# Decode attention with a dense block on one core: value sums in pairs, short last chunks, column output, and VectorE's scores by tensor_tensor_reduce

## The chip, the cores and the metric

The kernel runs on one core of one Trainium2 chip. Times are device microseconds (us) of that core. The kernel before takes 2061.26 us (median of 2 runs, 2060.8 to 2061.72). A difference counts as "faster" or "slower" when it is over 2%.

In the profile, PE is TensorE, PEld its weight load, DVE is VectorE, ACT is ScalarE, POOL is GpSimd, and SP is SyncE, which issues the loads here. L225 means line 225 of that kernel's file. The core's loads are shared by 16 DMA engines: the trace of before holds 8,616 landing records for 540 loads and stores, about 16 for each. What is said below of fetches, packets and landings is read from the traces.

## The reference, cut to what matters

```python
D, H, Sk, Dh, Dff = 640, 32, 32768, 192, 1536          # one query row, bf16
q = layernorm(x) @ wq                                   # [H, Dh]
scores = einsum("hd,hkd->hk", q, k_cache) * Dh ** -0.5  # k_cache [H, Sk, Dh]
p = softmax(scores)
o = einsum("hk,hkd->hd", p, v_cache)
h = x + o.reshape(H * Dh) @ wo
out = h + relu(layernorm(h) @ w1) @ w2
```

One query meets 32 heads of 32,768 keys and values. K and V are 32 x 32768 x 192 x 2 bytes x 2 = 805 MB; each is read once. Everything else is small.

## The kernel before

A chunk is 4,096 keys of one head: 128 partitions of 32 consecutive rows of 192 elements. There are 8 chunks a head, 256 in all. A K or V load is one DMA of 128 rows of 12,288 bytes.

```python
J = 32; CH = P * J; NC = Sk // CH      # 32 rows a partition, 4096 keys a chunk, 8 chunks a head
JP = 10; JD = J - JP                   # 10 rows' scores by PE, 22 by VectorE
kpool = ... bufs=5                     # five K tiles and five V tiles
...
def load_kv(g):
    h, c = divmod(g, NC)
    kt = kpool.tile([P, J * Dh], bf16, name="kt")
    nc.sync.dma_start(out=kt[:], in_=k_hd[h, c * CH:(c + 1) * CH, :].rearrange("(p j) d -> p (j d)", p=P))
    ...                                # the same for V
def scores_dve(g, mid=None):           # VectorE: one row of every partition per instruction (L225)
    ...
    for j in range(JD):
        if j == 4 and mid is not None:
            mid()                      # denominator of the head before
        st = scp.tile([P, Dh], bf16, name="st")
        nc.vector.scalar_tensor_tensor(out=st[:], in0=kt[:, j * Dh:(j + 1) * Dh], scalar=1.0, in1=qb[:],
                                       op0=A.mult, op1=A.mult, accum_out=sc[:, j:j + 1])
    return sc
def pv(g):                             # PE: value sums, one row per matmul (L245)
    ...
    for jj in range(J):
        ...
        nc.tensor.matmul(o[:], lhsT=p, rhs=vt[:, j * Dh:(j + 1) * Dh], ...)
...
for g in range(G):
    ...
    if c == 0 and h == H // 2:
        nc.sync.dma_start(out=w1_sb[:], in_=B_w1.rearrange("(c p) n -> p c n", p=P))
    if c == 0 and h == H // 2 + 1:
        nc.sync.dma_start(out=w2_sb[:], in_=B_w2.rearrange("(c p) n -> p c n", p=P))
    transposes(g)                      # PE turns the 10 rows that it scores itself: 15 transposes
    pv(g - 1); scores_pe(g); sc = scores_dve(g, ...); ...; exp_dve(g, sc)
```

The instruction streams are fully unrolled. The instructions themselves have to be fetched (248 packets on the two instruction queues, below).

The softmax here doesn't subtract the row's maximum and nothing guards it: scores larger than these inputs give would overflow.

## Time and profile before

| | before |
|---|---|
| time, span of the profiled run | 2061.26 us, 2060.4 us |
| VectorE busy, PE busy, ScalarE busy | 78%, 68%, 32% |
| granted TensorE clock (mean) | 0.835 |
| instruction fetches: queue 8 (16,384 B each), queue 14 (8,192 B each) | 130, 118 |
| last K or V packet ends | 2038.5 us |

The first fence is the page of the kernel before: busy time by engine, DMA rate in 40 equal slices, the two queues that carry instructions (packets, MB, share of 16 engines' span), and the group of VectorE's score instructions (busy us, mean ns, idle time before them and what ended it).

```profile
PE 1405.5 (68%) x16643; PEld 1193.5 (58%) x16643; DVE 1603.1 (78%) x11352; ACT 651.6 (32%) x1719; POOL 0.7 (0%) x6
...
GB/s 395 423 421 420 423 421 423 407 422 420 423 422 357 423 418 423 416 346 425 382 420 344 418 423 421 423 423 393 425 421 422 414 350 423 420 423 417 397 412 77
...
q8 instruction: 130, 2.13, 0.4%
q14 instruction: 118, 0.97, 0.1%
...
L225 DVE SCALAR_TENSOR_TENSOR st<-kt,qb 128x192 bf16<-128x192 bf16 x5632 | 1589.7, 350 | 306.7 <-DMA kt<-in_A_k_cache_dram 294.7
```

No compute engine is full, and what VectorE's score instructions wait for is nearly always K (294.7 of 306.7 us), so the loads look like the limit. (VectorE is idle 457 us in all; 132.8 us of the rest is a wait for PE, shown below.) Yet they are not always at 423 GB/s: there are holes (357, 346, 344, 350). The table by stretches shows what a hole is; its columns are the stretch, its length, busy time and instruction count of PE, PEld, DVE, ACT and POOL, the granted clock, the DMA share and GB/s.

```profile
1040.00:1060.00 20.00, 14.24 (x175) 11.83 (x172) 14.91 (x106) 5.51 (x17) 0.00 (x0) 0.83 1.01 422
1080.00:1100.00 20.00, 12.32 (x160) 10.75 (x157) 14.49 (x103) 5.50 (x15) 0.00 (x0) 0.84 0.57 212
...
2020.00:2040.00 20.00, 14.73 (x165) 12.47 (x166) 17.06 (x121) 6.63 (x14) 0.00 (x0) 0.83 0.07 27
```

At 1080 us the rate halves, and from 2020 to 2040 us, with the last K and V still on their way, it is 27 GB/s: 423 / 16 = 26.4, the rate of one engine. Fifteen of the 16 DMA engines have finished their shares and one has not. The landing records of the last K load show the same: 15 of its 16 lie between 2013.34 and 2015.21 us, the last at 2035.28, and PE's work on it starts at 2035.33. So it is the last share that lets the compute engines start. With five tiles of each kind, the 15 others run ahead until no tile is free, and then stand idle: SyncE's queue waits 247.2 us for VectorE's scores before K loads and 208.4 us for PE's value sums before V loads. The single packets in the trace confirm this: over the whole kernel, 36.3 us pass before the last K or V packet in which at most one of the 16 engines moves data.

The chain of waits that ended last shows the tail (start, duration, what):

```profile
2005.22 30.06 DMA kt<-in_A_k_cache_dram
2035.28 0.05 issue
2035.33 1.01 PE tp L195 x15
2036.34 4.34 PE o_ps L245 x32
...
2041.56 2.80 PE o_ps L245 x32
...
2047.57 1.79 PE y_a L336 x8
...
2057.30 0.23 PE y_a L346
```

The last K lands at 2035.28 us and 25.1 us of dependent work follow. The waits of VectorE (us in total, times, longest) and a piece of its timeline (start, duration) complete the picture:

```profile
DVE st L225 <- DMA kt<-in_A_k_cache_dram: 294.7, 181, 5.7
DVE rec L258 <- PE den L252: 132.8, 32, 5.9
```

```profile
1000.16 0.35 DVE L225 SCALAR_TENSOR_TENSOR st<-kt,qb 128x192 bf16<-128x192 bf16 x1
1000.44 0.08 DVE L225 DVE_READ_ACCUMULATOR st<-kt,qb 128x1 f32 x1
1000.44 0.35 DVE L225 SCALAR_TENSOR_TENSOR st<-kt,qb 128x192 bf16<-128x192 bf16 x1
```

One score instruction of the program appears as two, the operation and a read of the accumulator, and one score starts 279 ns after the other (its pitch, the median over the trace). So 22 rows take 6.1 us of a chunk.

### The profile page before, as it was taken

How to read it: one execution, taken by the hardware profiler on the slowest of the kernel's cores; microseconds unless marked ns; L12 is line 12 of the kernel's file. 1: busy time of each engine (PE TensorE's matmuls, PEld its weight loads, DVE VectorE, ACT ScalarE, POOL GpSimd, SP SyncE). 2: the span in 40 equal slices, each digit the busy share in tenths (PEclk: the TensorE clock that was granted, in tenths of full speed). 3: DMA queues.
4: the chain of work that ended last, by engine and by line, in shares of the span. 5: the costliest groups of instructions: out<-in, count | busy, mean ns of one | idle time of the engine just before them, and what ended most of it. 6: DMA issues, size and time to landing. Idle time of an engine off the chain costs nothing. (4 is left out here: it accounts for less than half of the span.)

```text
span 2060.4 us, 48468 instructions
## 1 busy us (share of the span) xinstructions
PE 1405.5 (68%) x16643; PEld 1193.5 (58%) x16643; DVE 1603.1 (78%) x11352; ACT 651.6 (32%) x1719; POOL 0.7 (0%) x6
## 2 busy tenths in 40 slices
PE   5766666766667666666665666766677667677767
PEld 4555555655555555555555555555566556566555
DVE  6877887778787788777777778887778877788775
ACT  3333333333333233322322333332333323333332
POOL 0000000000000000000000000000000000000000
PEclk9888887788898788888888888898788987878787
DMA  9999999999999999989998999999999989999991
GB/s 395 423 421 420 423 421 423 407 422 420 423 422 357 423 418 423 416 346 425 382 420 344 418 423 421 423 423 393 425 421 422 414 350 423 420 423 417 397 412 77
DMA packets 87844, 828.10 MB, mean 402 GB/s; under 512 B 8619, under 2 KB 21420, under 8 KB 22060
## 3 DMA queue, kind: packets, MB, share of 16 engines
q1 hardware_dynamic: 87596, 825.00, 96.5%
q8 instruction: 130, 2.13, 0.4%
q14 instruction: 118, 0.97, 0.1%
HBM read 824.97 MB, written 0.00 MB: 400 GB/s over the span
## 5 line engine op out<-in xcount | busy, mean ns | idle before, releaser
L225 DVE SCALAR_TENSOR_TENSOR st<-kt,qb 128x192 bf16<-128x192 bf16 x5632 | 1589.7, 350 | 306.7 <-DMA kt<-in_A_k_cache_dram 294.7
L195 PE MATMUL tp<-ident_b,kt 128*128 128x128 bf16 x3840 | 335.3, 255 | 596.6 <-DMA kt<-in_A_k_cache_dram 596.6
L195 PEld LDWEIGHTS <-kt 128*128 128x128 bf16 x3840 | 280.5, 116 | 623.8 <-DMA kt<-in_A_k_cache_dram 623.8
L245 PE MATMUL o_ps<-vt,pA 128*1 128x192 bf16 x5632 | 606.0, 272 | 45.8 <-ACT pA L232 45.6
L245 PEld LDWEIGHTS <-pA 128*1 128x1 bf16 x5632 | 524.9, 95 | 106.4 <-ACT pA L232 55.9
L196 ACT COPY kT<-tp 128x1024 bf16<-128x1024 bf16 (+1 forms) x512 | 465.1, 960 | 347.6 <-PE tp L195 347.3
L225 DVE DVE_READ_ACCUMULATOR st<-kt,qb 128x1 f32 x5632 | 442.4, 79 | 0.1
L245 PE MATMUL o_ps<-vt,pB 128*1 128x192 bf16 x2560 | 354.6, 305 | 0.4 <-ACT pB L212 0.4
L245 PEld LDWEIGHTS <-pB 128*1 128x1 bf16 x2560 | 237.2, 101 | 73.2 <-issue 22.8
L212 ACT ACTIVATE pB<-sp 128x10 bf16<-128x10 f32 x256 | 46.3, 181 | 630.9 <-PE sp L209 627.3
L232 ACT ACTIVATE pA<-sc 128x22 bf16<-128x22 f32 x256 | 56.6, 221 | 397.0 <-DVE st L225 396.8
L205 PEld LDWEIGHTS <-kT 128*128 128x128 bf16 x1280 | 100.0, 96 | 44.2 <-issue 43.3
L205 PE MATMUL sp<-qm,kT 128*128 128x2 bf16 x1280 | 122.3, 166 | 0.4 <-ACT kT L196 0.4
L209 PE MATMUL sp<-qm,kT 128*128 128x1 bf16 x1280 | 118.8, 163 | 0.4 <-ACT kT L196 0.4
L207 PE MATMUL sp<-qm,kT 128*128 128x1 bf16 x1280 | 118.7, 163 | 0.0
L258 DVE TENSOR_REDUCE rec<-den 1x1 f32<-1x16 f32 x32 | 5.2, 162 | 132.8 <-PE den L252 132.8
L207 PEld LDWEIGHTS <-kT 128*128 128x128 bf16 x1280 | 102.6, 96 | 0.0
L209 PEld LDWEIGHTS <-kT 128*128 128x128 bf16 x1280 | 101.4, 95 | 0.5 <-ACT kT L196 0.5
L212 ACT ACTIVATION_READ_ACCUMULATOR pB<-sp 128x1 f32 x256 | 49.9, 195 | 0.1
L232 ACT ACTIVATION_READ_ACCUMULATOR pA<-sc 128x1 f32 x256 | 48.1, 188 | 0.1
L163 PE MATMUL qps<-wq,xn_ln 128*1 128x192 bf16 x160 | 18.7, 248 | 3.3 <-DMA wq<-in_A_wq_dram 3.3
L265 ACT ACTIVATE o_pair<-o_ps,rec 1x192 f32<-1x192 f32 x32 | 13.2, 413 | 8.3 <-DVE rec L259 8.3
(62 smaller groups left out, 145.8 us busy)
## 6 DMA issues: line engine op xcount, KB each, us to landing
kt<-in_A_k_cache_dram SPq DMA_DIRECT2D x256, 1536.0 KB, 30.5
vt<-in_A_v_cache_dram SPq DMA_DIRECT2D x256, 1536.0 KB, 29.0
wq<-in_A_wq_dram SPq DMA_DIRECT2D x8, 960.0 KB, 27.1
wo<-in_A_wo_dram SPq DMA_DIRECT2D x16, 480.0 KB, 28.2
w_sb<-in_B_w_dram SPq DMA_DIRECT2D x2, 1920.0 KB, 32.2
x_row<-in_A_x_dram SPq DMA_DIRECT2D x1, 1.2 KB
out_dram<-y_row SPq DMA_DIRECT2D x1, 1.2 KB
```

The lines of the kernel that those rows point to most:

```text
L163: nc.tensor.matmul(qps[:], lhsT=xnT[:, c:c + 1], rhs=wq[:, c, hh * Dh:(hh + 1) * Dh], start=(c == 0), stop=(c == DT - 1))
L195: nc.tensor.transpose(out=tp[:, b, :], in_=kt[:, off:off + P], identity=ident_b[:])
L196: nc.scalar.copy(out=kT[:, b0:b0 + nb, :], in_=tp[:, 0:nb, :])
L205: nc.tensor.matmul(sp[:, 2 * i:2 * i + 2], lhsT=kT[:, 3 * i + 1, :], rhs=qm[:, 1:3], start=True, stop=False, skip_group_check=True)
L207: nc.tensor.matmul(sp[:, 2 * i:2 * i + 1], lhsT=kT[:, 3 * i, :], rhs=qm[:, 0:1], start=False, stop=False, skip_group_check=True)
L209: nc.tensor.matmul(sp[:, 2 * i + 1:2 * i + 2], lhsT=kT[:, 3 * i + 2, :], rhs=qm[:, 3:4], start=False, stop=True, skip_group_check=True)
L212: nc.scalar.activation(out=pB[:], in_=sp[:], func=F.Exp, scale=SCALE, accum_out=dsums[:, h, 2 * c + 1:2 * c + 2])
L225: nc.vector.scalar_tensor_tensor(out=st[:], in0=kt[:, j * Dh:(j + 1) * Dh], scalar=1.0, in1=qb[:], op0=A.mult, op1=A.mult, accum_out=sc[:, ...
L232: nc.scalar.activation(out=pA[:], in_=sc[:], func=F.Exp, scale=SCALE, accum_out=dsums[:, h, 2 * c:2 * c + 1])
L245: nc.tensor.matmul(o[:], lhsT=p, rhs=vt[:, j * Dh:(j + 1) * Dh], start=(c == 0 and jj == 0), stop=(c == NC - 1 and jj == J - 1))
L258: nc.vector.reduce_sum(out=s[:, 0:1], in_=d[:], axis=mybir.AxisListType.X)
L265: nc.scalar.activation(out=o_pair[(h // 2) % 2][0:1, (h % 2) * Dh:(h % 2 + 1) * Dh], in_=o[:], func=F.Copy, scale=s[0:1, 1:2])
```

## The change

The intent is to halve PE's value matmuls (two rows to a matmul, 384 columns wide, of which the matching halves are used), to hand VectorE four more rows a chunk by `tensor_tensor_reduce` (26 instead of 22, so PE transposes 6 rows instead of 10), to shorten the tail by splitting the last K and V rows into smaller chunks and producing the output as a column, and to take w1 in quarters of 120 + 8 partitions. The last point presumably aims at the lagging DMA engine.

```diff
-    JP = 10
-    JD = J - JP
+        parts = [(J, 6)] * NC                       # (rows a partition, rows scored by PE)
+        if h == H - 1:
+            parts = [(J, 6)] * (NC - 2) + [(J, 10), (16, 6), (8, 4), (8, 4)]
...
-                if j == 4 and mid is not None:
+                if j == 2 and mid is not None:
...
-                nc.vector.scalar_tensor_tensor(out=st[:], in0=kt[:, j * Dh:(j + 1) * Dh], scalar=1.0, in1=qb[:],
-                                               op0=A.mult, op1=A.mult, accum_out=sc[:, j:j + 1])
+                nc.vector.tensor_tensor_reduce(out=st[:], in0=kt[:, j * Dh:(j + 1) * Dh], in1=qb[:], scale=1.0,
+                                               scalar=0.0, op0=A.mult, op1=A.add, accum_out=sc[:, j:j + 1])
...
-            for jj in range(J):
...
-                nc.tensor.matmul(o[:], lhsT=p, rhs=vt[:, j * Dh:(j + 1) * Dh],
+            order = list(range(JD, jc, 2)) + list(range(0, JD, 2))
+            for i, j in enumerate(order):
+                p = pA[:, j:j + 2] if j < JD else pB[:, j - JD:j - JD + 2]
+                nc.tensor.matmul(o[:], lhsT=p, rhs=vt[:, j * Dh:(j + 2) * Dh],
...
-            if c == 0 and h == H // 2:
-                nc.sync.dma_start(out=w1_sb[:], in_=B_w1.rearrange("(c p) n -> p c n", p=P))
-            if c == 0 and h == H // 2 + 1:
+            if c == 2 and h >= H // 2 and h < H // 2 + 4:
+                i = h - H // 2
+                n1 = Dff // 4
+                w1_view = B_w1.rearrange("(c p) n -> p c n", p=P)
+                nc.sync.dma_start(out=w1_sb[0:120, :, i * n1:(i + 1) * n1], in_=w1_view[0:120, :, i * n1:(i + 1) * n1])
+                nc.sync.dma_start(out=w1_sb[120:P, :, i * n1:(i + 1) * n1], in_=w1_view[120:P, :, i * n1:(i + 1) * n1])
+            if c == 2 and h == H // 2 + 4:
                 nc.sync.dma_start(out=w2_sb[:], in_=B_w2.rearrange("(c p) n -> p c n", p=P))
...
-        for f in range(FT):                          # second dense matmul, a row of 640: 24 wide matmuls
-            nc.tensor.matmul(y_a[:], lhsT=h1T[:, f:f + 1], rhs=w2_sb[:, f, 0:512], ...
+        for n in range(DT):                          # the same as a column: 60 one-column matmuls
+            for f in range(FT):
+                nc.tensor.matmul(yps[:, n:n + 1], lhsT=w2_sb[:, f, n * P:(n + 1) * P], rhs=h1T[:, f:f + 1], ...
```

More of the change, by code (lines that the diff above doesn't have):

```diff
@@ L41 @@
     J = 32
-    CH = P * J
-    NC = Sk // CH
-    G = H * NC
-    JP = 10
-    JD = J - JP
-    NB = JP * Dh // P
-    QG = 4
-    assert Sk % CH == 0 and 2 * Dh == 3 * P and JP % 2 == 0 and H % QG == 0 and H % 2 == 0
+    QG = 4
+    assert Sk % (P * J) == 0 and 2 * Dh == 3 * P and H % QG == 0 and H % 2 == 0
+    NC = Sk // (P * J)
+    chunks = []
+    for h in range(H):
+        parts = [(J, 6)] * NC
+        if h == H - 1:
+            parts = [(J, 6)] * (NC - 2) + [(J, 10), (16, 6), (8, 4), (8, 4)]
+        k0 = 0
+        for c, (jc, jp) in enumerate(parts):
+            chunks.append((h, c, k0, jc, jp))
+            k0 += P * jc
+        assert k0 == Sk
+    G = len(chunks)
+    NCH = [sum(1 for q in chunks if q[0] == h) for h in range(H)]
+    NCM = max(NCH)
+    NBM = max(q[4] for q in chunks) * Dh // P
     const = ctx.enter_context(tc.tile_pool(name="const", bufs=1))
@@ L94, in load_kv @@
     def load_kv(g):
-        h, c = divmod(g, NC)
+        h, c, k0, jc, jp = chunks[g]
         kt = kpool.tile([P, J * Dh], bf16, name="kt")
-        nc.sync.dma_start(out=kt[:], in_=k_hd[h, c * CH:(c + 1) * CH, :].rearrange("(p j) d -> p (j d)", p=P))
+        nc.sync.dma_start(out=kt[:, 0:jc * Dh],
+                          in_=k_hd[h, k0:k0 + P * jc, :].rearrange("(p j) d -> p (j d)", p=P))
         vt = vpool.tile([P, J * Dh], bf16, name="vt")
-        nc.sync.dma_start(out=vt[:], in_=v_hd[h, c * CH:(c + 1) * CH, :].rearrange("(p j) d -> p (j d)", p=P))
+        nc.sync.dma_start(out=vt[:, 0:jc * Dh],
+                          in_=v_hd[h, k0:k0 + P * jc, :].rearrange("(p j) d -> p (j d)", p=P))
         kt_t[g], vt_t[g] = kt, vt
@@ L110 @@
     nc.vector.memset(ones_row[:], 1.0)
-    ones_col = const.tile([P, 1], f32)
+    ones_col = const.tile([P, 2], f32)
     nc.vector.memset(ones_col[:], 1.0)
@@ L119 @@
         nc.vector.memset(r[:], 0.0)
-    dsums = const.tile([P, H, 2 * NC], f32)
+    dsums = const.tile([P, H, 2 * NCM], f32)
+    nc.vector.memset(dsums[:], 0.0)
     w1_sb = const.tile([P, DT, Dff], bf16)
     w2_sb = const.tile([P, FT, D], bf16)
-    o_pair = [const.tile([1, 2 * Dh], f32, name=f"o_pair{i}") for i in range(2)]
+    o_pair = [const.tile([2, 2, 2 * Dh], f32, name=f"o_pair{i}") for i in range(2)]
     attT = aps.tile([P, DT], f32, name="attT")
@@ L188, in transposes @@
             kt = kt_t[g]
-            kT = tsb.tile([P, NB, P], bf16, name="kT")
+            h, c, k0, jc, jp = chunks[g]
+            NB = jp * Dh // P
+            kT = tsb.tile([P, NBM, P], bf16, name="kT")
             for b0 in range(0, NB, 8):
@@ L193, in transposes @@
                 for b in range(nb):
-                    off = JD * Dh + (b0 + b) * P
+                    off = (jc - jp) * Dh + (b0 + b) * P
                     nc.tensor.transpose(out=tp[:, b, :], in_=kt[:, off:off + P], identity=ident_b[:])
@@ L200, in scores_pe @@
             kT = kT_t.pop(g)
-            h, c = divmod(g, NC)
+            h, c, k0, jc, JP = chunks[g]
             qm = qm_t[h]
-            sp = sps.tile([P, JP], f32, name="sp")
+            sp = sps.tile([P, J], f32, name="sp")
             for i in range(JP // 2):
@@ L210, in scores_pe @@
                                  start=False, stop=True, skip_group_check=True)
-            pB = pcp.tile([P, JP], bf16, name="pB")
-            nc.scalar.activation(out=pB[:], in_=sp[:], func=F.Exp, scale=SCALE,
+            pB = pcp.tile([P, J], bf16, name="pB")
+            nc.scalar.activation(out=pB[:, 0:JP], in_=sp[:, 0:JP], func=F.Exp, scale=SCALE,
                                  accum_out=dsums[:, h, 2 * c + 1:2 * c + 2])
@@ L217, in scores_dve @@
             kt = kt_t.pop(g)
-            h, c = divmod(g, NC)
+            h, c, k0, jc, jp = chunks[g]
+            JD = jc - jp
             qb = qb_t[h]
-            sc = scp.tile([P, JD], f32, name="sc")
+            sc = scp.tile([P, J], f32, name="sc")
             for j in range(JD):
-                if j == 4 and mid is not None:
+                if j == 2 and mid is not None:
                     mid()
                 st = scp.tile([P, Dh], bf16, name="st")
-                nc.vector.scalar_tensor_tensor(out=st[:], in0=kt[:, j * Dh:(j + 1) * Dh], scalar=1.0, in1=qb[:],
-                                               op0=A.mult, op1=A.mult, accum_out=sc[:, j:j + 1])
+                nc.vector.tensor_tensor_reduce(out=st[:], in0=kt[:, j * Dh:(j + 1) * Dh], in1=qb[:], scale=1.0,
+                                               scalar=0.0, op0=A.mult, op1=A.add, accum_out=sc[:, j:j + 1])
             return sc
         def exp_dve(g, sc):
-            h, c = divmod(g, NC)
-            pA = pcp.tile([P, JD], bf16, name="pA")
-            nc.scalar.activation(out=pA[:], in_=sc[:], func=F.Exp, scale=SCALE,
+            h, c, k0, jc, jp = chunks[g]
+            JD = jc - jp
+            pA = pcp.tile([P, J], bf16, name="pA")
+            nc.scalar.activation(out=pA[:, 0:JD], in_=sc[:, 0:JD], func=F.Exp, scale=SCALE,
                                  accum_out=dsums[:, h, 2 * c:2 * c + 1])
@@ L236, in pv @@
         def pv(g):
-            h, c = divmod(g, NC)
+            h, c, k0, jc, jp = chunks[g]
+            JD = jc - jp
             vt, pA, pB = vt_t.pop(g), pA_t.pop(g), pB_t.pop(g)
             if c == 0:
-                o_t[h] = ops.tile([1, Dh], f32, name="o_ps")
+                o_t[h] = ops.tile([2, 2 * Dh], f32, name="o_ps")
             o = o_t[h]
-            for jj in range(J):
-                j = jj + JD if jj < JP else jj - JP
-                p = pA[:, j:j + 1] if j < JD else pB[:, j - JD:j - JD + 1]
-                nc.tensor.matmul(o[:], lhsT=p, rhs=vt[:, j * Dh:(j + 1) * Dh],
-                                 start=(c == 0 and jj == 0), stop=(c == NC - 1 and jj == J - 1))
+            order = list(range(JD, jc, 2)) + list(range(0, JD, 2))
+            for i, j in enumerate(order):
+                p = pA[:, j:j + 2] if j < JD else pB[:, j - JD:j - JD + 2]
+                nc.tensor.matmul(o[:], lhsT=p, rhs=vt[:, j * Dh:(j + 2) * Dh],
+                                 start=(c == 0 and i == 0), stop=(c == NCH[h] - 1 and i == len(order) - 1))
         den_t = {}
         def den_mm(h):
-            d = mm_bank([1, 2 * NC], f32, "den")
+            d = mm_bank([2, 2 * NCM], f32, "den")
             nc.tensor.matmul(d[:], lhsT=ones_col[:], rhs=dsums[:, h, :], start=True, stop=True)
@@ L256, in den_rec @@
             d = den_t.pop(h)
-            s = small.tile([1, 2], f32, tag="rec", name="rec")
+            s = small.tile([2, 2], f32, tag="rec", name="rec")
             nc.vector.reduce_sum(out=s[:, 0:1], in_=d[:], axis=mybir.AxisListType.X)
@@ L260, in den_rec, with o_scale @@
             den_t[h] = s
-        def o_scale(h):
+        def o_scale(h, last=False):
             s = den_t.pop(h)
             o = o_t.pop(h)
-            nc.scalar.activation(out=o_pair[(h // 2) % 2][0:1, (h % 2) * Dh:(h % 2 + 1) * Dh], in_=o[:],
-                                 func=F.Copy, scale=s[0:1, 1:2])
+            dst = o_pair[(h // 2) % 2]
+            n0 = (h % 2) * Dh
+            nc.scalar.activation(out=dst[:, 0, n0:n0 + Dh], in_=o[:, 0:Dh], func=F.Copy, scale=s[:, 1:2])
+            if last:
+                nc.vector.tensor_scalar_mul(out=dst[:, 1, n0:n0 + Dh], in0=o[:, Dh:2 * Dh], scalar1=s[:, 1:2])
+            else:
+                nc.scalar.activation(out=dst[:, 1, n0:n0 + Dh], in_=o[:, Dh:2 * Dh], func=F.Copy, scale=s[:, 1:2])
         oT_t = {}
         def o_turn(pr):
+            src = o_pair[pr % 2]
             ps = mm_bank([P, 3], f32, "oT_ps")
             for b in range(3):
-                nc.tensor.transpose(out=ps[:, b:b + 1], in_=o_pair[pr % 2][0:1, b * P:(b + 1) * P],
-                                    identity=ident_f[0:1, 0:1])
+                for i in range(2):
+                    nc.tensor.matmul(ps[:, b:b + 1], lhsT=src[:, i, b * P:(b + 1) * P], rhs=ident_f[0:2, i:i + 1],
+                                     start=(i == 0), stop=(i == 1))
             oT = small.tile([P, 3], bf16, tag="oT", name="oT")
@@ L290 @@
         for g in range(G):
-            h, c = divmod(g, NC)
+            h, c, k0, jc, jp = chunks[g]
             if g > 0:
@@ L320 @@
             exp_dve(g, sc)
-        pv(G - 1)
         den_mm(H - 1)
         den_rec(H - 1)
-        o_scale(H - 1)
+        pv(G - 1)
+        o_scale(H - 1, last=True)
         o_turn(H // 2 - 1)
@@ L331 @@
         hnT = layernorm_col(h_col, "ln2")
-        y_a = ops.tile([1, 512], f32, tag="o_ps", name="y_a")
-        y_b = ops.tile([1, P], f32, tag="o_ps", name="y_b")
-        for c in range(DT):
-            y = y_a[0:1, c * P:(c + 1) * P] if c < 4 else y_b[0:1, :]
-            nc.tensor.matmul(y, lhsT=h_col[:, c:c + 1], rhs=ident_f[:], start=(c == 0 or c == 4),
-                             stop=False, skip_group_check=True)
-        h1ps = mm_bank([P, FT], f32, "h1ps")
+        h1ps = ops.tile([P, FT], f32, tag="o_ps", name="h1ps")
         for f in range(FT):
@@ L344 @@
         nc.scalar.activation(out=h1T[:], in_=h1ps[:], func=F.Relu)
-        for f in range(FT):
-            nc.tensor.matmul(y_a[:], lhsT=h1T[:, f:f + 1], rhs=w2_sb[:, f, 0:512],
-                             start=False, stop=(f == FT - 1), skip_group_check=True)
-            nc.tensor.matmul(y_b[:], lhsT=h1T[:, f:f + 1], rhs=w2_sb[:, f, 512:D],
-                             start=False, stop=(f == FT - 1), skip_group_check=True)
-        y_row = small.tile([1, D], bf16, tag="y_row", name="y_row")
-        nc.scalar.copy(out=y_row[0:1, 0:512], in_=y_a[:])
-        nc.vector.tensor_copy(out=y_row[0:1, 512:D], in_=y_b[:])
-        nc.sync.dma_start(out=out.rearrange("b s d -> (b s) d"), in_=y_row[:])
+        yps = ops.tile([P, DT], f32, tag="o_ps", name="yps")
+        for n in range(DT):
+            for f in range(FT):
+                nc.tensor.matmul(yps[:, n:n + 1], lhsT=w2_sb[:, f, n * P:(n + 1) * P], rhs=h1T[:, f:f + 1],
+                                 start=(f == 0), stop=(f == FT - 1))
+        y_col = small.tile([P, DT], f32, tag="y_col", name="y_col")
+        nc.vector.tensor_add(out=y_col[:], in0=h_col[:], in1=yps[:])
+        ytp = mm_bank([DT, P], f32, "ytp")
+        nc.tensor.transpose(out=ytp[:], in_=y_col[:], identity=ident_f[:])
+        y_row = small.tile([DT, P], bf16, tag="y_row", name="y_row")
+        nc.vector.tensor_copy(out=y_row[:], in_=ytp[:])
+        nc.sync.dma_start(out=out.rearrange("b s (c p) -> (b s c) p", p=P), in_=y_row[:])
 _INS = ['A_x', 'A_k_cache', 'A_v_cache', 'A_wq', 'A_wo', 'B_x', 'B_w1', 'B_w2']
```

## The prediction

> **What bounds the kernel now.** DMA, but not all 16 engines. The slice table shows DMA at 9 tenths and 420-423 GB/s almost everywhere; 825 MB at 423 GB/s would take 1950 us, yet the last K tile lands at 2035 us (chain of waits). The stretch table shows 27 GB/s from 2020 to 2040 us, one engine's rate (423/16 = 26.4), with similar holes at 640-660 and 1080-1100 us. So one DMA engine lags; the rest run out of free tiles and wait. The single packets of the trace say why. A K/V packet (12,288 B) takes 464 ns. The instruction fetches of queue 14 (8,192 B, 118 of them) each hold one K/V packet up by 588 ns on average, and at 2018 us, when a single engine is left, that engine is the one held up (464 to 1,120 ns). 118 x 588 ns = 69 us, about the lag. Queue 8 (130 fetches, PE's 33,100 instructions x 64 B) sits on another engine; queue 14 fits DVE + ACT + SP (15,100 x 64 B, each score operation counted twice for its accumulator read).
>
> DVE is busy 78%: 22 score operations a chunk start 279 ns apart (timeline), 6.14 us of a 7.95 us chunk. At each head it waits 4.15 us for the denominator (132.8 us / 32, waits). PE is 68% busy, ACT 32%.
>
> **The change.**
> - PE: 15 to 9 transposes, 32 to 16 value matmuls a chunk (twice as wide), instructions 33,100 to 19,000. Off the critical path: no gain in the main loop.
> - DVE: 26 operations a chunk, by tensor_tensor_reduce. It still issues two instructions each. [...] the trace has 279 ns for the old operation. I estimate 279 to 285 ns: 26 x 0.28 = 7.3 us, plus 3.3 us per head / 8 = 0.4: 7.7 us a chunk against a DMA pace of 7.95. DVE just hides.
> - Instruction fetches on queue 14: 15,100 to 17,300 instructions, 135 packets, +10 us on the lagging engine. [...] Net: last K lands near 2039 us.
> - Tail, 25.1 us from the last K landing to the end (chain): the value matmuls after it (9 us) shrink to about 4.5; the h_col matmuls (2.2 us) go; the second MLP matmul (5.8 us) becomes about 2.4 with its transpose. About 15 us remain: 10 saved.
>
> **Time.** 2039 + 15, plus 1 as before between span and measured time: about 2056 us, range 2030 to 2110. Chances: faster by over 2% 0.05, within 0.75, slower 0.20.
>
> **What would show it.** tensor_tensor_reduce starts 279-285 ns apart; DVE busy over 90% (1,850 us or more); chunk starts still ended by the K DMA; queue 14 near 135 packets, queue 8 near 74; 12-17 us after the last K landing.
>
> **What would make it wrong.** The new operation's pitch. At about 290 ns DVE becomes the limit (2030 us = 6,656 x pitch + 31 x 3.3 us); every further 10 ns cost 67 us, so 300 ns gives about 2115 us and 330 ns 2310 us. This trace has no reading of it. [...] if another queue sits on the lagging engine too, up to 30 us less.

The forecast's sum was 2061 us before, -10 (tail), +10 (fetches) and -5 (w1): 2056 us. Its w1 term: that a load of 120 partitions keeps off one DMA engine is not shown by any trace here. The 2039 us for the last K and the 2056 us contain the term; without it the sum is 2061 us.

The 64 bytes of an instruction follow from the page of before: 130 fetches x 16,384 bytes / (16,643 matmuls + 16,643 weight loads) = 64.0.

## The result, and the profile after

The changed kernel takes 2087.11 us (2086.72 and 2087.5), 1.0126 of the time before (95% interval 1.0102 to 1.0151): within 2%, but 26 us longer. All outputs are right. A ratio here is the mean time of one kernel's runs over that of the other's of the same rounds, so it is not quite the ratio of the medians quoted.

The page of the changed kernel, in the same lines:

```profile
PE 1380.5 (66%) x9682; PEld 688.5 (33%) x9682; DVE 1878.2 (90%) x13379; ACT 495.4 (24%) x1759; POOL 0.7 (0%) x6
...
GB/s 396 423 421 422 422 422 424 384 421 422 419 387 365 424 417 405 401 369 423 343 416 383 358 397 413 340 423 419 424 422 423 415 356 424 416 413 382 419 387 131
...
q8 instruction: 75, 1.23, 0.2%
q14 instruction: 135, 1.11, 0.1%
...
L242 DVE CUSTOM_DVE_ANT_0 st<-kt,qb 128x192 bf16<-128x192 bf16 x6644 | 1864.5, 345 | 65.3 <-DMA kt<-in_A_k_cache_dram 62.7
```

PE lost 42% of its instructions, and VectorE rose to 90%. The granted TensorE clock fell from 0.835 to 0.777. That alone does not explain the loss: of the runs below, a_w1quarters is 12 us faster than the change at nearly its clock (0.789), and b_dve_more 14 us slower than the kernel before at the same clock (0.835). The slices have more holes than before, above all in the middle, where w1 is loaded. The table by stretches of the changed kernel shows the same picture of a single late engine near the end (198 GB/s, then 13 in a stretch whose loads end half-way):

```profile
2040.00:2060.00 20.00, 13.68 (x100) 6.92 (x99) 20.00 (x145) 4.65 (x17) 0.00 (x0) 0.76 0.55 198
2060.00:2080.00 20.00, 16.15 (x195) 10.02 (x194) 11.94 (x83) 7.68 (x27) 0.00 (x0) 0.84 0.04 13
```

The end of its chain of waits:

```profile
2068.04 0.20 ACT pB L228
2068.25 0.04 issue
2068.29 1.46 PE o_ps L265 x8
...
2072.40 0.67 PE o_ps L265 x4
...
2078.14 1.75 PE h1ps L366 x60
...
2080.15 1.75 PE yps L373 x60
```

The last K lands at 2068.1 us by the trace's landings, and 16.8 us of work follow it, where it was 25.1. So the tail gained 8.3 us, and the main loop lost 33. VectorE's waits and its timeline:

```profile
DVE rec L278 <- PE den L272: 128.2, 32, 5.9
DVE st L242 <- DMA kt<-in_A_k_cache_dram: 62.7, 51, 5.6
```

```profile
999.98 0.34 DVE L242 CUSTOM_DVE_ANT_0 st<-kt,qb 128x192 bf16<-128x192 bf16 x1
1000.25 0.07 DVE L242 DVE_READ_ACCUMULATOR2_ANT sc<- 128x1 f32 x1
1000.25 0.34 DVE L242 CUSTOM_DVE_ANT_0 st<-kt,qb 128x192 bf16<-128x192 bf16 x1
```

The trace lists `tensor_tensor_reduce` as CUSTOM_DVE_ANT_0 and its accumulator read as DVE_READ_ACCUMULATOR2_ANT; of both, only the times and counts measured here are used. The new operation starts every 279 ns (median), just as the old one, and it too reads its accumulator in a second instruction (6,644 of each, 345 and 74 ns in the mean; the old one before had 350 and 79 ns).

### A closer look at the lagging engine, without a new run

The trace of the kernel before holds every DMA packet and landing. The interval between the last landings of successive K and V loads (511 intervals) is the pace of the slowest engine. Sorted by the instruction fetches that began in each interval (four more had two fetches of queue 14):

```
fetches in the interval   intervals   median length
none                      311         3.697 us
one of queue 8             86         3.697 us
one of queue 14            68         4.666 us
one of each                42         4.666 us
```

A fetch of queue 14 makes the interval 0.97 us longer; one of queue 8 leaves it as it was. Of 98 intervals with one queue-14 fetch and no other load in them, 69 were longer by 0.85 to 1.2 us and 24 were not longer at all (under 0.12 us), with 5 in between. So most queue-14 fetches, not all, seem to be made by the lagging DMA engine. What they do there is visible too: the fetch takes about 330 ns, and the K/V packet after it 1,120 instead of 464 ns; 330 + 656 = 986 ns, about the 0.97 us. Of the 118 fetches, 70 are followed by a packet of 1,120 ns.

Whose are they? A fetch is 8,192 bytes, which is 128 instructions of 64 bytes (b_dve_more and b_pool_more below add 2,048 and 8,192 instructions and show 16 and 64 fetches more). VectorE has 5,982 instructions in the program and 5,632 accumulator reads, 11,614 together, or 91 fetches of the 118. By the same count the remaining 27 belong to ScalarE and SyncE. This was an inference from counts (91 of 118 is 77%, the longer intervals 69 of 98 or 70%); the runs below test it.

### The profile page after: what moved, and what is told of

It reads as the page before. It is cut to its first block, busy times and chain, and to the rows that moved or that the text cites. A ratio compares the mean times of both kernels' runs of the same rounds, so it can differ in the third digit from the quotient of the medians.

```text
span 2084.9 us, 36636 instructions
## 1 busy us (share of the span) xinstructions
PE 1380.5 (66%) x9682; PEld 688.5 (33%) x9682; DVE 1878.2 (90%) x13379; ACT 495.4 (24%) x1759; POOL 0.7 (0%) x6
## 5 line engine op out<-in xcount | busy, mean ns | idle before, releaser
L242 DVE CUSTOM_DVE_ANT_0 st<-kt,qb 128x192 bf16<-128x192 bf16 x6644 | 1864.5, 345 | 65.3 <-DMA kt<-in_A_k_cache_dram 62.7
L265 PE MATMUL o_ps<-vt,pA 128*2 128x384 bf16 x3322 | 841.4, 423 | 183.2 <-ACT pA L250 182.3
L265 PEld LDWEIGHTS <-pA 128*2 128x2 bf16 x3322 | 339.6, 105 | 677.0 <-issue 325.6
L211 PE MATMUL tp<-ident_b,kt 128*128 128x128 bf16 x2322 | 219.1, 254 | 507.8 <-DMA kt<-in_A_k_cache_dram 507.4
L242 DVE DVE_READ_ACCUMULATOR2_ANT sc<- 128x1 f32 x6644 | 492.1, 74 | 0.0
L211 PEld LDWEIGHTS <-kt 128*128 128x128 bf16 x2322 | 166.0, 114 | 531.9 <-DMA kt<-in_A_k_cache_dram 530.9
L212 ACT COPY kT<-tp 128x1024 bf16<-128x1024 bf16 (+2 forms) x514 | 301.5, 637 | 106.8 <-PE tp L211 106.2
L265 PE MATMUL o_ps<-vt,pB 128*2 128x384 bf16 x774 | 219.2, 403 | 0.1
L278 DVE TENSOR_REDUCE rec<-den 2x1 f32<-2x20 f32 x32 | 5.3, 167 | 128.2 <-PE den L272 128.2
L221 PEld LDWEIGHTS <-kT 128*128 128x128 bf16 x774 | 62.6, 96 | 102.5 <-issue 100.8
L223 PE MATMUL sp<-qm,kT 128*128 128x1 bf16 x774 | 81.1, 163 | 0.0
L225 PE MATMUL sp<-qm,kT 128*128 128x1 bf16 x774 | 81.1, 163 | 0.0
L223 PEld LDWEIGHTS <-kT 128*128 128x128 bf16 x774 | 65.1, 97 | 0.0
L225 PEld LDWEIGHTS <-kT 128*128 128x128 bf16 x774 | 63.9, 96 | 0.0
```

The lines of the kernel that those rows point to most:

```text
L211: nc.tensor.transpose(out=tp[:, b, :], in_=kt[:, off:off + P], identity=ident_b[:])
L212: nc.scalar.copy(out=kT[:, b0:b0 + nb, :], in_=tp[:, 0:nb, :])
L221: nc.tensor.matmul(sp[:, 2 * i:2 * i + 2], lhsT=kT[:, 3 * i + 1, :], rhs=qm[:, 1:3], start=True, stop=False, skip_group_check=True)
L223: nc.tensor.matmul(sp[:, 2 * i:2 * i + 1], lhsT=kT[:, 3 * i, :], rhs=qm[:, 0:1], start=False, stop=False, skip_group_check=True)
L225: nc.tensor.matmul(sp[:, 2 * i + 1:2 * i + 2], lhsT=kT[:, 3 * i + 2, :], rhs=qm[:, 3:4], start=False, stop=True, skip_group_check=True)
L242: nc.vector.tensor_tensor_reduce(out=st[:], in0=kt[:, j * Dh:(j + 1) * Dh], in1=qb[:], scale=1.0, scalar=0.0, op0=A.mult, op1=A.add, accum ...
```

## The experiments

The theory: the time is set by one DMA engine, which also fetches VectorE's instructions. VectorE's instructions went from 11,614 to 13,643 by the change (16 more fetches), and this costs about 16 us.
Rivals: VectorE itself, at 90%, has become the limit (its slower pitch, or the 128 us of waits for the denominator); the cut of w1 at partition 120 costs time; or all instruction fetches, whoever's, cost alike.

### Undoing one part of the change at a time

**w1 and w2 as before, in one load each**

```diff
-            if c == 2 and h >= H // 2 and h < H // 2 + 4:
-                ...                       # four quarters, each cut in 120 + 8 partitions
-            if c == 2 and h == H // 2 + 4:
+            if c == 0 and h == H // 2:
+                nc.sync.dma_start(out=w1_sb[:], in_=B_w1.rearrange("(c p) n -> p c n", p=P))
+            if c == 0 and h == H // 2 + 1:
```

> The changed kernel with w1 and w2 loaded as before: w1 in one DMA of 128 partitions and 3072 B rows at head 16, w2 at head 17, instead of eight DMAs of 120 and 8 partitions with 768 B rows over heads 16 to 19. Theory A (the split w1 load costs time: its 768 B packets take as long as 1280 B ones, and it takes eight of the places in the DMA queue): about 2076 us, 8 to 13 us less than the changed kernel's 2087. Theory B (the split relieves the lagging engine by 5 us, and the loss lies elsewhere): 2087 to 2093 us.

Measured: 2076.81 us, 1.0066 of before (1.0049 to 1.0082). The cut of w1 costs about 10 us, where the prediction had counted it as a gain of 5.

**The old score operation in the changed kernel**

```diff
-                nc.vector.tensor_tensor_reduce(out=st[:], in0=..., in1=qb[:], scale=1.0,
-                                               scalar=0.0, op0=A.mult, op1=A.add, accum_out=sc[:, j:j + 1])
+                nc.vector.scalar_tensor_tensor(out=st[:], in0=..., scalar=1.0, in1=qb[:],
+                                               op0=A.mult, op1=A.mult, accum_out=sc[:, j:j + 1])
```

> The changed kernel with scalar_tensor_tensor in place of tensor_tensor_reduce, all else kept. Theory A (the new operation has the same pitch, 280 against 279 ns, and the same two instructions): 2085 to 2090 us, queue 14 still near 135 fetches. Rival (the new operation costs time that its pitch does not show, for instance by its waits): 2060 to 2075 us.

Measured: 2087.03 us, 1.0118 (1.0103 to 1.0133), the same as the change. Its timeline has the same pitch:

```profile
1000.02 0.34 DVE L242 SCALAR_TENSOR_TENSOR st<-kt,qb 128x192 bf16<-128x192 bf16 x1
1000.30 0.07 DVE L242 DVE_READ_ACCUMULATOR st<-kt,qb 128x1 f32 x1
1000.30 0.34 DVE L242 SCALAR_TENSOR_TENSOR st<-kt,qb 128x192 bf16<-128x192 bf16 x1
```

The choice of the operation makes no difference that these runs can show (1.0118 against 1.0126).

**Ten rows by PE, 22 by VectorE, as before**

```diff
-        parts = [(J, 6)] * NC
+        parts = [(J, 10)] * NC
...                                        # and the same in the last head's list
```

> The changed kernel with 10 rows of a chunk scored on PE as before, so 22 on VectorE instead of 26. Theory A (VectorE's 26 operations plus the wait at each head leave no slack, and its 2 x 4 x 250 more instructions add 16 fetches to queue 14): 2060 to 2072 us, VectorE busy near 1600 us, queue 14 near 119 fetches; of this about 10 us by fetches and 7 us or more by slack. Rival (the loss lies in the value sums or the w1 loads): 2080 to 2088 us.

Measured: 2068.0 us, 1.0027 (1.0012 to 1.0042); queue 14 back to 119 fetches. Handing VectorE four rows more a chunk costs 19 us. This run alone does not say whether by VectorE's time or by its fetches.

**The denominator later in the chunk, so that VectorE does not wait for it**

```diff
-                if j == 2 and mid is not None:
+                if j == 16 and mid is not None:
```

> The changed kernel with VectorE's denominator work after score 16 of the head's first chunk instead of after score 2, so it no longer waits for PE there (128 us of waits, 4.0 us a head). Theory A1 (VectorE is the limit in most of the run): 60 to 100 us of waits gone and 20 us or more less, 2067 us or below. Theory A2 (VectorE is only a near second to the lagging DMA engine): 3 to 12 us less, 2075 to 2084 us, with VectorE's waits for K growing by about what the head waits lose.

Measured: 2084.89 us, 1.011 (1.0095 to 1.0125). VectorE's waits in this run:

```profile
DVE st L242 <- DMA kt<-in_A_k_cache_dram: 152.4, 112, 5.7
DVE rec L278 <- PE den L272: 22.0, 21, 2.1
```

106 us of waits were taken from VectorE, and 2 us came off the time, somewhat less than expected; the waits for K rose by 90 us. VectorE was waiting for the same thing in another place. It is a near second, not the limit.

### Whose fetches, and which loads

These kernels add to the kernel *before* instructions that compute nothing of use.

**32 GpSimd instructions more a chunk (8,192, or 64 fetches)**

```diff
...                                        # junk: an own tile of 32 columns
+            for i in range(32):
+                nc.gpsimd.memset(junk[:, i:i + 1], 0.0)
```

> The kernel before with 8192 one-column memsets on the idle GpSimd engine, which nothing waits for: 64 more instruction fetches of 8192 B if they go through queue 14. Theory A (fetches on queue 14 delay the one lagging DMA engine, which sets the time): 64 x 0.617 us = 39 us more, 2095 to 2106 us. Rival (the lag has another cause, fetches only coincide with it): 2058 to 2066 us.

Measured: 2069.11 us, 1.0037 (1.0022 to 1.0052). The page shows the fetches, on queue 14, and the group shows the added work:

```profile
q14 instruction: 182, 1.49, 0.2%
```

```profile
L222 POOL MEMSET junk<- 128x1 f32 x8192 | 273.8, 98 | 39.0 <-POOL junk L222 35.0
```

64 more fetches on the same queue cost 8 us, not 62: more than the rival expected, far less than theory A. The intervals show why. GpSimd waits for nothing and is done with its instructions at 314 us. Up to 320 us, 39 of 51 intervals with a queue-14 fetch are longer by 0.55 to 0.8 us, not by 0.97, and the third to sixth slices fall to 416, 367, 404 and 343 GB/s; the K and V loads are then 29 us behind those of the kernel before. From 320 to 725 us none of 19 such intervals is longer, and the delay shrinks to 12 us; after that the 0.97 us are back, and 8 us remain at the end. This fits one reading: GpSimd's fetches make another DMA engine late, and while that one is behind, the engine of VectorE's fetches loses nothing that counts. So the queue's number is not the cause. On this reading, which the records do not prove because they do not name the DMA engine, it matters whose instructions are fetched, since that decides which DMA engine is delayed; delays of different DMA engines overlap, and the most delayed one sets the time.

**16 PE instructions more a chunk (4,096 matmuls with their weight loads, or 32 fetches of 16,384 bytes)**

```diff
...                                        # the tile sp is 16 columns wider
+            for i in range(16):
+                nc.tensor.matmul(sp[:, JP + i:JP + i + 1], lhsT=ones_row[:], rhs=ones_row[0:1, 0:1],
+                                 start=True, stop=True, skip_group_check=True)
```

> The kernel before with 16 one-column matmuls more a chunk on PE (8192 instructions with their weight loads, the same number of bytes to fetch as in b_pool_more) through queue 8. Theory A (only queue 14 is on the lagging engine): 2059 to 2072 us, with 32 more fetches on queue 8. Rival (any instruction bytes cost the same DMA time): 2090 to 2105 us.

Measured: 2062.44 us, 1.0005 (0.9988 to 1.0022), no difference, with the fetches there:

```profile
q8 instruction: 162, 2.65, 0.5%
```

PE's fetches cost nothing that shows, so the change's saving of 55 of them should gain nothing. They are not small: in the trace of before a queue-8 fetch takes 1,069 ns and the K/V packet after it 954 instead of 464 ns (medians), an estimated 1.56 us together. All 130 on one DMA engine would be 203 us, while the loads end only 64 us later than in b_tt below (2038.5 against 1974.4 us); so, as an estimate, they are spread over several. The records do not say over how many.

**8 VectorE instructions more a chunk (2,048, or 16 fetches: as many as the change adds)**

```diff
...                                        # junk: an own tile of 8 columns
+            for i in range(8):
+                nc.vector.memset(junk[:, i:i + 1], 0.0)
```

> The kernel before with 8 one-column memsets a chunk on VectorE, which nothing waits for: as many more VectorE instructions (2048, 16 fetches) as the change's 4 more scores a chunk bring, for about 0.5 us of its 1.8 us of idle time a chunk. The GpSimd run has cut the theory down: only fetches for VectorE sit on the lagging engine. Theory A (so it is; in the trace of before a fetch either delays the last landing by 0.97 us or not at all): 16 x 0.97 = 15 us more, 2073 to 2080 us. Rival (fetches cost nothing, as the GpSimd run could also be read): 2059 to 2065 us.

Measured: 2075.76 us, 1.0069 (1.0054 to 1.0084), 14.2 us more, with

```profile
q14 instruction: 134, 1.10, 0.1%
```

That is 0.89 us for each of 16 fetches, against 0.97 us read from the intervals. The instructions themselves take 59 ns each, 0.47 us of a chunk in which VectorE was idle over a fifth of the time. In the packets, the last K or V packet ends at 2052.4 us instead of 2038.5: the loads became later, not the work after them. 81 intervals with one queue-14 fetch are longer by 0.85 to 1.2 us, where before it was 69.

**Other loads of the kernel before, cut at partition 120**

```diff
-        nc.sync.dma_start(out=t[:], in_=wq_view[:, :, ...])
+        for lo, hi in ((0, 120), (120, P)):
+            nc.sync.dma_start(out=t[lo:hi], in_=wq_view[lo:hi, :, ...])
...                                        # and the same for wo
```

> The kernel before with each load of wq and wo cut at partition 120, as the change cuts w1, row sizes kept. Theory A [...]: its 44 us of weight packets go, 2020 to 2045 us. Theory B (the lagging engine is another one): no gain, 2062 to 2085 us, a few us for 24 more loads.

Theory A is that the cut relieves the lagging DMA engine of its share of these loads.

Measured: 2148.37 us, 1.0425 (1.0407 to 1.0442): 24 cuts cost 87 us, beyond both expectations.

**w1 in four quarters, but uncut**

```diff
-                nc.sync.dma_start(out=w1_sb[0:120, :, ...], in_=w1_view[0:120, :, ...])
-                nc.sync.dma_start(out=w1_sb[120:P, :, ...], in_=w1_view[120:P, :, ...])
+                nc.sync.dma_start(out=w1_sb[:, :, ...], in_=w1_view[:, :, ...])
```

> The changed kernel with w1 still in four loads of 768 B rows over heads 16 to 19, but each over all 128 partitions. It tells the two halves of the w1 change apart; w1 whole gave 2077 us, the change 2087. Theory A (the cut at 120 partitions costs the time): 2075 to 2080 us. Theory B (the 768 B rows cost it): 2083 to 2090 us. Theory C (the cut relieves the lagging engine and the rows cost more than it gains): above 2090 us.

Measured: 2075.35 us, 1.0068 (1.0053 to 1.0083), the same as w1 in one load. So the quarters, with their 768-byte rows, are free, and the cut alone costs 10 to 12 us. The packet records of the four kernels show one reason, in median packet times:

```
load and packet         whole    cut at 120
w1, 768 bytes           36 ns    56 ns       (a_w1quarters; the change)
wo, 1,280 bytes         55 ns    82 ns       (before; b_w120)
wq, 1,536 bytes         65 ns    120 ns      (before; b_w120)
K and V, mean           470.7    479.3 ns    (before; b_w120, where K and V are not cut)
```

As an estimate from these medians and means, spread evenly over 16 engines: wq has 8 x 640 packets and wo 16 x 384, so 5,120 x 55 ns / 16 + 6,144 x 27 ns / 16 = 28 us, and 65,536 K/V packets x 8.6 ns / 16 = 35 us, together 63 of the 87 us. The other 24 us, and why packets get slower, are not shown. The two runs measure the cost of loading 120 and 8 partitions in place of 128: 10 to 12 us for four cuts and 87 us for 24.

### The same scores with a tenth of VectorE's instructions

If VectorE's fetches are the cost, taking them away must gain even where VectorE gets busier. This kernel is the one before with its 22 score instructions a chunk (44 with the accumulator reads) replaced by two multiplies and two sums over 11 rows each; the denominator's work comes between the two halves, and the pool of these tiles has two buffers instead of three.

```diff
-            for j in range(JD):
-                ...
-                nc.vector.scalar_tensor_tensor(..., accum_out=sc[:, j:j + 1])
+            half = JD // 2
+            for a in (0, half):
+                ...
+                pr = scp.tile([P, (JD // 2) * Dh], bf16, name="pr")
+                prv = pr[:, 0:half * Dh].rearrange("p (j d) -> p j d", d=Dh)
+                nc.vector.tensor_tensor(out=prv, in0=kt[:, a * Dh:(a + half) * Dh].rearrange("p (j d) -> p j d", d=Dh),
+                                        in1=qb[:].unsqueeze(1).to_broadcast([P, half, Dh]), op=A.mult)
+                nc.vector.tensor_reduce(out=sc[:, a:a + half], in_=prv, op=A.add, axis=mybir.AxisListType.X)
```

> The kernel before with VectorE's 22 scores of a chunk made by two multiplies and two reductions over 11 rows each (4 instructions instead of 44; products rounded to bf16). VectorE's work time stays about the same, 6.5 to 7.3 us a chunk; its fetches nearly vanish, so queue 14 falls from 118 to 30 or fewer. Theory A (VectorE's fetches are the 80 to 90 us by which one DMA engine lags): 20 to 50 us less, 2010 to 2043 us, then held by the engine that fetches for PE. Rival (fetches do not matter): 2058 to 2070 us.

Measured: 2001.2 us, 0.9707 (0.9693 to 0.9722), faster by 3%. Its page:

```profile
PE 1396.8 (70%) x16643; PEld 1177.6 (59%) x16643; DVE 1826.0 (91%) x1112; ACT 647.9 (32%) x1719; POOL 0.7 (0%) x6
...
GB/s 397 423 422 420 425 421 424 420 423 422 422 423 419 424 424 423 422 419 425 420 420 389 419 424 422 423 424 419 424 422 423 422 420 423 423 422 424 421 424 137
...
q14 instruction: 38, 0.31, 0.0%
...
L229 DVE TENSOR_REDUCE sc<-pr 128x11 f32<-128x2112 bf16 x512 | 1204.7, 2353 | 35.8 <-ACT kT L196 0.9
L227 DVE TENSOR_TENSOR pr<-kt,qb 128x2112 bf16<-128x2112 bf16 x512 | 639.5, 1249 | 58.6 <-DMA kt<-in_A_k_cache_dram 45.6
```

A row now takes (1249 + 2353) / 11 = 327 ns of VectorE in place of 280 (7.2 us a chunk, within the 6.5 to 7.3 expected), and VectorE is as busy as in the change (91%), yet the kernel is 60 us faster than before and 86 us faster than the change. Eighty fetches are gone, and with them the holes: the time with at most one DMA engine active before the last K or V packet falls from 36.3 to 0.1 us, and that packet ends at 1974.4 us instead of 2038.5. The time is below the range of theory A. With a_late_den, this rules VectorE's busy time out as the limit of the change. Of the 38 fetches left, 11 are VectorE's by count (1,373 instructions), and 10 are followed by a packet of 1,120 ns, where it was 70 of 118: an estimated 60 x 0.97 = 58 us less on the late engine. The last packet came 64 us earlier. Most slices now stand at 419 to 425 GB/s, so the 16 engines together seem to be the limit then. The products are rounded to bf16 before they are summed; the result stayed correct.

### The good parts together

**The change with ten PE rows and w1 whole**: the edits of a_jp10 and a_w1whole together.

> The changed kernel with both its losses undone: 10 rows a chunk on PE, w1 and w2 whole. Pair sums, short last chunks, column output and tensor_tensor_reduce stay. Theory A (the two losses are separate and add up: 19 and 10 us): 2055 to 2061 us, a little under the kernel before by its shorter tail. Rival (both runs took away the same loss): 2064 to 2070 us.

Measured: 2056.84 us, 0.9978 (0.9962 to 0.9995), 4.5 us below before. This is what the pairs of value rows, the short last chunks and the column output are worth.

**The same with the batched scores**: the edits of b_tt on top of it (the products' tile is 11 rows wide throughout).

> The run above with the four-instruction scores of b_tt: pair sums also cut PE's fetches from 130 to about 99. Theory A: faster than both kernels and than b_tt, 2000 to 2035 us. Rival (fetches do not matter): 2054 to 2065 us.

Measured: 1989.09 us (1987.92 to 1989.84), 0.9648 (0.9634 to 0.9663). Its page:

```profile
PE 1403.8 (71%) x12730; PEld 806.4 (41%) x12730; DVE 1825.5 (92%) x1123; ACT 657.2 (33%) x1759; POOL 0.7 (0%) x6
...
GB/s 395 423 422 421 424 421 425 422 422 423 422 425 420 423 424 422 424 419 424 421 423 399 421 423 423 422 424 420 424 423 424 423 420 423 423 423 424 423 424 216
```

It beats the kernel before by 72 us and the change by 98, more than theory A expected.

## Why the prediction was right or wrong

The time, 2087.1 us, is within the range (2030 to 2110), the class "within 2%" had the largest chance, and the direction of the central value was wrong: 2056 was below the time before, the result is above it. The range was 80 us wide, so it is in part luck that the result lies in it. The prediction's sum was -10 us (tail) + 10 (fetches) - 5 (w1); the steps measured below are -4.5, +18.1 and +12.4. Of the 31 us by which it fell short, w1 makes 17, the four rows 8 and the rest 5.5. Point by point:

- **"One DMA engine lags; the rest run out of free tiles and wait."** Right, and the basis of everything. When the fetches go, the lag goes (b_tt: 36.3 to 0.1 us with at most one DMA engine active).
- **tensor_tensor_reduce at 279 to 285 ns, VectorE over 90% or 1,850 us.** Right: 279 ns, and 90%, 1,878 us. The largest risk named ("the new operation's pitch") did not come true, and a_stt shows that the operation made no difference.
- **Queue 14 near 135, queue 8 near 74.** Right: 135 and 75.
- **"Instruction fetches on queue 14: ... 135 packets, +10 us on the lagging engine."** The mechanism was right and its size was off. The prediction divided all fetches of the queue evenly (588 ns each). The intervals show 0.97 us for a fetch on the lagging engine and none for the others, and the fetches that the change adds are VectorE's, which are those that count: 16 x 0.97 = 15.5 us; measured alone, 14.2 us (b_dve_more). The prediction put ScalarE's and SyncE's fetches on that engine too; GpSimd's, added on the same queue, made intervals longer by 0.65 instead of 0.97 us and delayed what seems to be another DMA engine (b_pool_more), and of the 118 fetches only 70 show the long packet, so fetches of one queue do not all fall on one DMA engine.
- **w1 in 120 + 8 partitions gains 5 us.** The author's estimate rested on the assumption that the cut relieves the lagging DMA engine, which is not shown, and it was wrong in sign. The cut costs 10 to 12 us (a_w1whole, a_w1quarters), and b_w120 shows a cost on other loads too (87 us for 24 cuts). The risk stated with it (cut too) was only 5 us more and left the packets' own time as it was, whereas it rose from 36 to 56 ns.
- **"PE: ... Off the critical path: no gain in the main loop."** Right. In the packets, the last K or V packet of a_jp10_w1whole ends at 2039.1 us, against 2038.5 before; b_pe_more shows that PE's fetches cost nothing.
- **"DVE just hides", with 3.3 us of wait per head.** Nearly. The wait was 128.2 / 32 = 4.0 us per head. Taking it away gained 2 us (a_late_den), so VectorE is not the limit, but not far below it.
- **"About 15 us remain: 10 saved."** 16.8 remain of 25.1 after the last K landing: 8.3 saved.

The steps from before to the change, each with the two ratios that bracket it, and the end of the last K or V packet in the traces:

```
kernel                               ratio     step       last K/V packet
before                               1                    2038.5 us
+ pairs, short chunks, column out    0.9978    -4.5 us    2039.1 us   (a_jp10_w1whole)
+ four rows from PE to VectorE       1.0066    +18.1 us   2059.7 us   (a_w1whole)
+ w1 in quarters, cut at 120         1.0126    +12.4 us   2068.6 us   (the change)
```

A step is the difference of the ratios times 2061.3 us. The runs are of three batches, so a step has an uncertainty of some 3 to 5 us. Of the 18 us, an estimated 14 to 15.5 are the fetches (the two figures above). The rest, some 3 to 4 us, is within the uncertainty, though the packets give 20.5 us for the step, and was not isolated; that VectorE at 90% has less room to catch up after a hole is a guess. What stays open besides is over how many DMA engines PE's fetches are spread, whether a load of 120 partitions leaves one out and whether that is the late one, and why the packets of a cut load are slower.

## What to carry to other kernels

Where DMA slices show holes and the rate at the end of the loads is a sixteenth of the full rate, look at the packets of the instruction queues. Here the fetches shared DMA engines with the data (the K/V packet after most queue-14 fetches took 1,120 instead of 464 ns), and VectorE's many small instructions made one of 16 late for all: an estimated 70 x 0.97 = 68 us in the kernel before, of which b_tt won back 60. Delays of different DMA engines seem to overlap (b_pool_more: 64 fetches more, 8 us), so the instructions to save are those whose fetches fall on the latest one. Then fewer and longer instructions can beat cheaper ones, even if they make the compute engine busier, as here from 78% to 91% with 3% less time. And measure a trick that rests on which DMA engine a load takes by itself, before it is combined with others.
